# A linear-attention and gated-expert kernel: a new pipeline, k^T v per head in column tiles, and TensorE kept in program order

## The chip, the cores and the metric

The kernel runs on one core of a Trainium2 chip. Its time is the device time of one execution in microseconds (us); the figure quoted is the median of several runs. The traces come from the hardware profiler, one execution each. Five engines work side by side, each through its own instructions in a fixed order: TensorE (PE, with its weight loads as PEld), VectorE (DVE), ScalarE (ACT), GpSimd (POOL), and SyncE (SP), whose queue issues the DMAs here.

## What is computed

Two layers, one behind the other, for 8 batches of 576 tokens.

```python
kv = np.einsum('bhsd,bhse->bhde', k, v)            # 8 heads of 64, no softmax
out = np.einsum('bhsd,bhde->bhse', q, kv)
rms = np.sqrt(np.mean(out * out, axis=-1, keepdims=True) + 1e-06)
x = out / rms * g_norm                             # [8, 576, 512], heads side by side
logits = x @ w_gate                                # 4 experts, the best 2 of them kept
for e in range(E):                                 # w: softmax of the 2 kept logits
    q = x @ wq[e]; k = x @ wk[e]; v = x @ wv[e]    # head size 64
    a = softmax(causal(scale * (q @ k.transpose(0, 2, 1))))
    out += w[..., e] * (a @ v @ wo[e])
```

All four experts are computed for every token; the gate then weighs them.

## The kernel before

The work of a batch has two stages. **Stage 1** (`attention`) makes x. For each of four pairs of heads it transposes q into qT2_all (five blocks of tokens, 128, 128, 128, 128 and 64; `pe_transpose`, line 97), and multiplies k by v for the pair (line 177): a 128x128 product of which only the two 64x64 blocks on the diagonal are wanted. VectorE copies these into kv2_all (lines 186 and 187). Then, block by block of tokens, TensorE makes p_out (line 212, four products in fp32), ScalarE squares it (sq, line 220), VectorE sums (sumsq, line 222) and adds eps (msq, line 229), GpSimd raises to the power -0.5 (rstd, line 238), VectorE scales (x_tok, line 245), TensorE transposes back (p_xT, line 97 again), ScalarE copies it out, and VectorE makes the rounded copy xT_r.

**Stage 2** (`moe_block`) makes the gate from x (p_lt, line 266: fp32 products with only four weight columns, 512 and 64 tokens wide; then p_log, and small VectorE steps), v for all experts (p_v, line 322), and for each of two pairs of experts: q and k projected (p_proj, line 346), scores in causal strips (p_sc, line 371; the two experts of a pair stand in rows 0 to 63 and 64 to 127 and come one behind the other), their exponential (PT, line 378), the triangular mask on GpSimd (line 384), the product with v (p_O, line 409, with one extra column for the sum), its scaling (lines 417 and 418), and the transpose p_OT. The output product p_y (line 455, `moe_final`) of a batch is done within the next one.

`run_interleaved` puts steps of stage 1 of batch b+1 between those of stage 2 of batch b, one for every `ratio` steps. That is the order of the program only: a scheduler then orders each engine's instructions by its own estimates. PSUM, where products land, is one pool of eight one-bank buffers. Loads of a batch go out two batches ahead, in rows of 256 bytes, and the weights are loaded ahead of the first batch.

## Time and profile before

| | |
|---|---|
| median of 3 runs | 517.08 us (516.87 to 517.32) |
| span of the profiled execution | 515.2 us |
| TensorE busy | 400.2 us, 78% |
| VectorE, ScalarE, GpSimd busy | 197.3, 173.9, 124.2 us |
| mean granted TensorE clock | 0.838 of full speed |
| DMA | 40.31 MB, 78 GB/s over the span |

The time of a run is some 2 us more than the span, which goes from the first to the last instruction. Busy time of TensorE is modelled from the starts of its pipelined products: the distance between the starts of two groups tells more than the length of one. An fp32 product shows as two TensorE instructions (passes): 20 products of p_out a batch are 320 in eight batches. PEclk is the granted share of TensorE's clock: 1.00 is 2.4 GHz, 0.50 is 1.2 GHz.

### The profile page before, as it was taken

To read this page: it belongs to the slowest core of one execution; us is meant where nothing else is said; L and a number is where in the kernel's file an instruction comes from. 1 tells how busy PE (TensorE), PEld (TensorE's weight loads), DVE (VectorE), ACT (ScalarE), POOL (GpSimd) and SP (SyncE) were. 2 spreads that over 40 slices of the span, in tenths; PEclk is the share of its full clock that TensorE was granted. 3 is DMA by queue.
4 is the path that set the end of the run, shared out by engine and by line. 5 is a ranking of instruction groups with operands and counts; after the bars stand their busy time and mean duration, and the time that the engine had idled before them with its cause. 6 is when DMAs were issued, how large, how long until landed. Compare 5 with 4: busy or idle time off the path is not lost.

```text
span 515.2 us, 7111 instructions
## 1 busy us (share of the span) xinstructions
PE 400.2 (78%) x2472; PEld 285.5 (55%) x2472; DVE 197.3 (38%) x717; ACT 173.9 (34%) x569; POOL 124.2 (24%) x234
## 2 busy tenths in 40 slices
PE   0066696959969899679968799679968799679884
PEld 0055285726758467554757368454757367564661
DVE  1104334354252342543443442543433542543523
ACT  0013143611514215252246215251245215251440
POOL 3004202430132302351043302351043302340220
PEclk9999799869955599797988699796988699796866
DMA  8999908801390015900295014900200011000202
GB/s 168 206 195 204 206 13 160 118 1 42 108 205 15 2 41 128 199 2 0 92 182 96 1 41 119 207 3 0 87 7 1 1 42 52 0 2 1 93 0 92
DMA packets 125107, 40.31 MB, mean 78 GB/s; under 512 B 120208, under 2 KB 120208, under 8 KB 125072
## 3 DMA queue, kind: packets, MB, share of 16 engines
q1 hardware_dynamic: 125072, 39.87, 38.8%
q8 instruction: 19, 0.31, 0.3%
q14 instruction: 16, 0.13, 0.1%
HBM read 30.42 MB, written 9.44 MB: 77 GB/s over the span
## 4 chain that ended last, share of the span: by engine, by line
PE 56%; DVE 13%; POOL 11%; ACT 8%; issue 5%; DMA 3%; SPq 3%; POOLq 0%; DVEq 0%; ACTq 0%
POOL rstd L238 11%; PE p_kv L177 10%; PE p_lt L266 9%; PE p_proj L346 9%; PE p_out L212 5%; PE p_v L322 4%; PE p_qT L97 4%; DVE O_sc L418 4%; PE p_O L409 4%; PE p_y L455 3%; DVE x_tok L245 3%; PE p_sc L371 3%; ACT PT L378 3%; DVE sumsq L222 3%; ACT sq L220 2%
## 5 line engine op out<-in xcount | busy, mean ns | idle before, releaser
L384 POOL TENSOR_SCALAR_AFFINE_SELECT PT<-PT 128x128 bf16<-128x128 bf16 (+1 forms) x160 | 44.0, 290 | 195.4 <-ACT PT L378 191.0
L238 POOL TENSOR_TENSOR rstd<-msq,neg_half 128x8 f32<-128x8 f32 (+1 forms) x40 | 65.8, 1645 | 102.3 <-DVE msq L229 98.8
L378 ACT ACTIVATE PT<-p_sc 128x64 bf16<-128x64 f32 (+5 forms) x288 | 65.1, 341 | 14.5 <-PE p_sc L371 13.8
L409 PE MATMUL p_O<-vext,PT 128*128 128x65 bf16 (+2 forms) x480 | 43.5, 232 | 22.0 <-DVE x_tok L245 20.3
L371 PE MATMUL p_sc<-qTp,kTp 64*128 64x64 f32 (+5 forms) x288 | 49.3, 305 | 6.7 <-ACT kTp L358 4.2
L212 PE MATMUL p_out<-kv_all,qT_all 128*128 128x128 f32 (+1 forms) x320 | 52.8, 318 | 2.1 <-ACT PT L378 2.1
L245 DVE TENSOR_TENSOR x_tok<-p_out,rstd 128x512 f32<-128x512 f32 (+1 forms) x40 | 27.6, 689 | 65.3 <-POOL rstd L238 65.3
L177 PE MATMUL p_kv<-v_b,k_b 128*128 128x128 f32 (+1 forms) x320 | 51.7, 300 | 0.0
L97 PE MATMUL p_OT<-ident_b,O_sc 128*128 128x128 bf16 (+1 forms) x80 | 21.8, 273 | 38.4 <-DVE O_sc L418 38.1
L97 PE MATMUL p_qT<-ident_f,q_b 128*128 128x128 f32 (+1 forms) x160 | 28.6, 288 | 29.1 <-DMA q_b<-in_q_dram 29.1
L266 PE MATMUL p_lt<-xT,wg_f 128*4 128x64 f32 (+1 forms) x128 | 50.9, 564 | 0.0
L418 DVE TENSOR_SCALAR O_sc<-p_O,invr,gate 128x64 bf16<-128x64 f32 (+1 forms) x160 | 49.8, 334 | 1.6 <-PE p_OT L97 0.6
L409 PEld LDWEIGHTS <-PT 128*128 128x128 bf16 (+2 forms) x480 | 31.8, 124 | 30.8 <-POOL PT L384 11.1
L371 PEld LDWEIGHTS p_sc<-qTp,kTp 64*128 64x128 f32 (+1 forms) x288 | 39.3, 188 | 16.0 <-ACT kTp L358 5.8
L212 PEld LDWEIGHTS p_out<-kv_all,qT_all 128*128 128x128 f32 (+1 forms) x320 | 44.8, 209 | 5.8 <-ACT PT L378 3.5
L220 ACT ACTIVATE sq<-p_out 128x512 f32<-128x512 f32 (+1 forms) x40 | 23.8, 596 | 66.4 <-PE p_out L212 58.9
L222 DVE TENSOR_REDUCE sumsq<-sq 128x8 f32<-128x512 f32 (+1 forms) x40 | 27.2, 680 | 47.8 <-ACT sq L220 47.8
L177 PEld LDWEIGHTS p_kv<-v_b,k_b 128*128 128x128 f32 (+1 forms) x320 | 41.5, 194 | 6.3 <-issue 0.2
L174 ACT COPY qT_all<-p_qT 128x512 f32<-128x512 f32 x64 | 23.0, 419 | 61.5 <-PE p_qT L97 61.5
L186 DVE COPY kv_all<-p_kv 64x64 f32<-64x64 f32 x32 | 6.9, 216 | 90.1 <-PE p_kv L177 87.3
L97 PEld LDWEIGHTS p_qT<-ident_f,q_b 128*128 128x128 f32 (+1 forms) x160 | 19.4, 143 | 37.4 <-DMA q_b<-in_q_dram 19.9
L97 PE MATMUL p_xT<-ident_f,x_tok 128*128 128x128 f32 (+1 forms) x160 | 30.8, 330 | 8.7 <-DVE x_tok L245 5.8
(53 smaller groups left out, 419.9 us busy)
## 6 DMA issues: line engine op xcount, KB each, us to landing
q_b<-in_q_dram SPq DMA_DIRECT2D x32, 256.0 KB, 5.0
k_b<-in_k_dram SPq DMA_DIRECT2D x32, 256.0 KB, 5.0
v_b<-in_v_dram SPq DMA_DIRECT2D x32, 256.0 KB, 5.1
out_dram<-y_sb SPq DMA_DIRECT2D x32, 256.0 KB, 2.1
q_b<-in_q_dram SPq DMA_DIRECT2D x8, 128.0 KB, 5.1
k_b<-in_k_dram SPq DMA_DIRECT2D x8, 128.0 KB, 4.8
v_b<-in_v_dram SPq DMA_DIRECT2D x8, 128.0 KB, 4.4
out_dram<-y_sb SPq DMA_DIRECT2D x8, 128.0 KB, 2.3
```

Of the source, the lines that this page charges most:

```text
L97: nc.tensor.transpose(out_ap, in_ap, ident[:npart, :npart])
L177: nc.tensor.matmul(p_kv[:, :], lhsT=kb[:nt, i, 2 * hp : 2 * hp + 2, :].rearrange("p h d -> p (h d)"), rhs=vb[:nt, i, 2 * hp : 2 * hp + 2, ...
L212: nc.tensor.matmul(p_out[:nt, hp * P : (hp + 1) * P], lhsT=qT2_all[:, hp, t0 : t0 + nt], rhs=kv2_all[:, hp, :], start=True, stop=True,)
L238: nc.gpsimd.tensor_tensor(out=rstd[:nt, :], in0=msq[:nt, :], in1=neg_half[:nt, :], op=AluOpType.pow,)
L245: nc.vector.tensor_tensor(out=x_tok[:nt, :].rearrange("p (h d) -> p h d", h=H), in0=p_out[:nt, :].rearrange("p (h d) -> p h d", h=H), in1= ...
L266: nc.tensor.matmul(p_lt[:, :], lhsT=wg_f[:, c, :], rhs=xT_sb[:, c, slo:shi], start=(c == 0), stop=(c == NCH - 1),)
L346: nc.tensor.matmul(p_proj[:, :], lhsT=wsrc[:, c, 2 * pr : 2 * pr + 2, :].rearrange("p e f -> p (e f)"), rhs=xT_r[:, c, plo:phi], start=(c ...
L371: nc.tensor.matmul(p_sc[:nk, :], lhsT=kT_pair[pb : pb + Hd, t0 : t0 + nk], rhs=qT_pair[pb : pb + Hd, lo:hi], start=True, stop=True,)
L378: nc.scalar.activation(PT[:nk, off + (lo - t0) : off + (hi - t0)], p_sc[:nk, :], ACTF.Exp, scale=scale,)
L384: nc.gpsimd.affine_select(out=PT[:nk, off : off + nk], in_=PT[:nk, off : off + nk], compare_op=AluOpType.is_ge, fill=0.0, base=0, pattern= ...
L409: nc.tensor.matmul(p_O[:nq, :], lhsT=PT[:nkk, col : col + nq], rhs=v_ext[:nkk, kbi, e, :], start=(kbi == 0), stop=(kbi == qci),)
L418: nc.vector.tensor_scalar(out=O_sc[:nq, el, :], in0=p_O[:nq, 0:Hd], scalar1=invr[:nq], scalar2=gate[:nq, qci, e : e + 1], op0=AluOpType.mu ...
```

## The change

The kernel body is rewritten; shapes, data types and results stay. The core of the diff for stage 1 and the loads:

```diff
-    ps = ctx.enter_context(tc.tile_pool(name="ps", bufs=8, space=bass.MemoryType.PSUM))
...
+    ps2 = ctx.enter_context(tc.tile_pool(name="ps2", bufs=3, space=bass.MemoryType.PSUM))
+    ps1 = ctx.enter_context(tc.tile_pool(name="ps1", bufs=2, space=bass.MemoryType.PSUM))
+
+    def big(name):
+        return ps2.tile([P, 2, 512], FP32, tag="big", name=name)
+
+    def small(shape, name, dtype=FP32):
+        return ps1.tile(shape, dtype, tag="small", name=name)
...
+            main(kt, k, h0, h0 + step)
+            main(vt, v, h0, h0 + step)
+            if h0 == 0:
+                rem(kr[b % 2], k)
+                rem(vr[b % 2], v)
+        for i, (t0, nt) in enumerate(blocks):
+            nc.sync.dma_start(
+                qt[:nt, i, :, :], q[b, :, t0 : t0 + nt, :].rearrange("h p d -> p h d")
+            )
+        return qt, kt, vt
...
+    loads = {0: load_qkv(0, fine=True)}
...
+    def kv_pair(p_kv, c, kb, vb, krem, vrem):
+        for j in range(NF + 1):
+            for hh in range(2):
+                h = 2 * c + hh
+                lk, rv = (kb[:, h, j, :], vb[:, h, j, :]) if j < NF else (krem[:, h, :], vrem[:, h, :])
+                nc.tensor.matmul(
+                    p_kv[hh * Dh : (hh + 1) * Dh, c, :], lhsT=lk, rhs=rv,
+                    start=(j == 0), stop=(j == NF), skip_group_check=True,
+                )
+
+    def kv_copy(p_kv, kvb, kv2):
+        for hh in range(2):
+            pp = slice(hh * Dh, (hh + 1) * Dh)
+            nc.vector.tensor_copy(out=kvb[pp, :, hh, 0:Dh], in_=p_kv[pp, :, :])
+            nc.scalar.copy(kv2[pp, :, hh * Dh : (hh + 1) * Dh], p_kv[pp, :, :])
...
+        p_kv = small([P, NCH, Dh], "p_kv")
+        for c in range(NCH):
+            kv_pair(p_kv, c, kb, vb, kr[b % 2], vr[b % 2])
+        kv_copy(p_kv, kvb, kv2)
+        yield 4.3
...
+        p_kt = small([P, NCH, P], "p_kt")
+        for c in range(NCH):
+            nc.tensor.transpose(p_kt[:, c, :], kv2[:, c, :], ident_f[:])
+        kt_sb = s1.tile([P, NCH, P], FP32, tag="kvT", name="kvT")
+        nc.vector.tensor_copy(out=kt_sb[:], in_=p_kt[:])
+        yield 0.5
+        q_block(1)
+        yield 0.5
...
+        for c in range(NCH):
+            nc.tensor.matmul(
+                p_kg[:, c, :, :].rearrange("p a e -> p (a e)"),
+                lhsT=kt_sb[:, c, :],
+                rhs=wg_bd[:, c, :, :].rearrange("p a e -> p (a e)"),
...
+        nc.vector.tensor_copy(out=kvb[:, :, :, Dh:GW], in_=p_kg[:])
+        yield 0.9
...
-            p_kv = psum([P, P], name="p_kv")
-            for i, (t0, nt) in enumerate(blocks):
-                nc.tensor.matmul(
-                    p_kv[:, :],
-                    lhsT=kb[:nt, i, 2 * hp : 2 * hp + 2, :].rearrange(
...
-                    rhs=vb[:nt, i, 2 * hp : 2 * hp + 2, :].rearrange("p h d -> p (h d)"),
...
-            nc.vector.tensor_copy(kv2_all[0:Dh, hp, 0:Dh], p_kv[0:Dh, 0:Dh])
-            nc.vector.tensor_copy(kv2_all[Dh:P, hp, Dh:P], p_kv[Dh:P, Dh:P])
...
-            p_lt = psum([E, shi - slo], name="p_lt")
+            p_o = big("p_out")
             for c in range(NCH):
                 nc.tensor.matmul(
-                    p_lt[:, :],
-                    lhsT=wg_f[:, c, :],
-                    rhs=xT_sb[:, c, slo:shi],
-                    start=(c == 0),
-                    stop=(c == NCH - 1),
-                )
...
-            pe_transpose(p_log[:nt, i, :], lgT[:, t0 : t0 + nt], E)
...
+                    p_o[:nt, c // 2, (c % 2) * 2 * GW : (c % 2 + 1) * 2 * GW],
+                    lhsT=qT[:, c, t0 : t0 + nt],
+                    rhs=kvb[:, c, :, :].rearrange("p a g -> p (a g)"),
+                    start=True,
+                    stop=True,
+                )
...
+            sq = sqs[i % 3]
+            nc.scalar.activation(
+                sq[:nt, :, 0:Dh].rearrange("p (k h) d -> p k h d", k=2),
+                po[:, :, :, 0:Dh],
+                ACTF.Square,
+                scale=1.0 / (Dh**0.5),
...
+            ms = blk.tile([P, H], FP32, tag="ms", name="ms")
+            nc.vector.tensor_reduce(ms[:nt], sq[:nt], axis=AX_X, op=AluOpType.add)
+            rstd = blk.tile([P, H], FP32, tag="rstd", name="rstd")
+            nc.gpsimd.tensor_tensor(
+                out=rstd[:nt], in0=ms[:nt], in1=neg_half[:nt], op=AluOpType.pow
+            )
...
+            nc.vector.tensor_tensor(
...
+            gl = blk.tile([P, H, E], FP32, tag="gl", name="gl")
+            nc.vector.tensor_tensor(
...
+            nc.vector.tensor_reduce(
+                lg8[:nt, i, 0:E],
...
+            pend.append((i, xt))
+            yield 0.9
+            if len(pend) > 1:
+                x_flush()
+                yield 0.45
+        while pend:
+            x_flush()
+            yield 0.45
```

k and v of 512 tokens now come in rows of 1024 bytes, four tokens to a partition (the sum over tokens doesn't mind their order), the last 64 tokens in zero-filled tiles of their own, so every product of line 175 has 128 rows. There are 40 of them a batch instead of 20, each 64 weight columns by 64 moving columns, the heads of a pair in turns in the two column halves of the array. The gate's weights are folded in: p_kt transposes kv, p_kg multiplies by the gate weights, and p_out gets 136 columns instead of 128, the eight more of which are the logits per head; gl and lg8 scale and add them. p_lt, p_log, msq and the second copy of xT are gone. VectorE copies qT, ScalarE copies y.

Stage 2 computes the same products: the projections in two halves of 288 tokens instead of 512 and 64, 24 score products a batch instead of 36, the two experts of a pair in turns into two banks, so that one exponential serves both (10 a batch instead of 36) and one mask too (10 instead of 20). The rest, and what sets the order:

```diff
+            def piece(parts):
+                p_s = big("p_sc")
+                o = 0
+                for kb, lo, hi in parts:
+                    for el in range(2):
+                        pb = slice(el * Hd, (el + 1) * Hd)
                         nc.tensor.matmul(
...
+                            p_s[:, el, o : o + hi - lo],
+                            lhsT=kTp[pb, kb * P : (kb + 1) * P],
+                            rhs=qTp[pb, lo:hi],
...
+                d0 = strip_off[kb] + lo - kb * P
...
+        def pv(pr):
+            PT = res["PT", pr]
+            p_O = big("p_O")
...
+                for n, qc in enumerate(qcs):
...
+                for sub in ((qcs,) if bank == 0 else ((3,), (4,))):
...
+                    iv = inv[:nq, sub[0] : sub[0] + nn, :]
+                    nc.vector.reciprocal(iv.rearrange("p n e -> p (n e)").unsqueeze(2), po[:, :, Hd : Hd + 1])
+                    nc.vector.tensor_tensor(
+                        out=iv, in0=iv, in1=gate[:nq, sub[0] : sub[0] + nn, 2 * pr : 2 * pr + 2],
+                        op=AluOpType.mult,
...
+                    nc.vector.tensor_tensor(
+                        out=osc[:nq, sub[0] : sub[0] + nn, :, :].rearrange("p n e f -> p (n e) f"),
+                        in0=po[:, :, 0:Hd],
+                        in1=iv.rearrange("p n e -> p (n e)").unsqueeze(2).to_broadcast([nq, 2 * nn, Hd]),
+                        op=AluOpType.mult,
                     )
...
+        def o_t(pr):
+            osc = res["osc", pr]
+            p_t = small([P, S], "p_OT", BF16)
...
+                nc.tensor.transpose(
+                    p_t[:, s0 : s0 + nq],
+                    osc[:nq, qc, :, :].rearrange("p e f -> p (e f)"),
...
+            nc.scalar.copy(OT[:, pr, :], p_t[:])
+            yield 0.5
+
+        yield from proj(0)
+        yield from scores(0)
+        yield from proj(1)
+        yield from scores(1)
+        if prev_y is not None:
+            yield from prev_y
+        yield from pv(0)
+        yield from o_t(0)
+        yield from pv(1)
+        yield from o_t(1)
+        res["OT"] = OT
...
+            p_y = small([P, D], "p_y")
...
+            nc.scalar.copy(y[:nq, :], p_y[:nq, :])
...
+    W1, W2 = 16.0, 17.0
+
+    def weave(main, side):
+        a = s = 0.0
+        live = side is not None
+        for c in main:
+            a += c / W2
+            while live and s < a:
                 try:
-                    next(gen_side)
+                    s += next(side) / W1
...
+    with tc.manual_schedule(engines={mybir.EngineType.PE}):
...
+            weave(stage2(b, res, y_gen), stage1(b + 1, nxt) if b + 1 < B else None)
```

`weave` goes by the costs that the steps yield. `manual_schedule` keeps TensorE's instructions in program order; the other engines are still ordered by the scheduler. PSUM is now three buffers of two banks (big) and two of one bank (small).

Three places show the new order, each before and then changed. First VectorE in stage 1 of a batch while stage 2 of the one before it runs (invr, O_sc and osc belong to stage 2). Before:

```order
L222 TENSOR_REDUCE sumsq<-sq 128x8
L417 RECIPROCAL invr<-p_O 128x1 x2
L229 SCALAR_TENSOR_TENSOR msq<-sumsq,eps_row 128x8
L418 TENSOR_SCALAR O_sc<-p_O,invr,gate 128x64
L245 TENSOR_TENSOR x_tok<-p_out,rstd 128x512
L418 TENSOR_SCALAR O_sc<-p_O,invr,gate 128x64
L222 TENSOR_REDUCE sumsq<-sq 128x8
```

Changed, for the second and third block of a batch:

```order
L266 TENSOR_REDUCE ms<-sq_120 128x8
L273 TENSOR_TENSOR x_tok<-p_out,rstd 128x512
L280 TENSOR_TENSOR gl<-p_out,rstd 128x32
L286 TENSOR_REDUCE lg_0_102<-gl 128x4
L308 MAX m_2312<-lg_0_102 128x8
L446 RECIPROCAL inv<-p_O 128x6
L266 TENSOR_REDUCE ms<-sq_122 128x8
L447 TENSOR_TENSOR inv<-inv,gate 128x6
L451 TENSOR_TENSOR osc<-p_O,inv 128x384
L273 TENSOR_TENSOR x_tok<-p_out,rstd 128x512
```

In both, the sum for a block stands behind x_tok of the block ahead of it; three small steps of the gate now stand between them.

Second, TensorE at the end of stage 1 of batch 0. Before:

```order
L212 MATMUL p_out<-kv_all,qT_all 128x128 x4
L97 MATMUL p_xT<-ident_f,x_tok 128x128 x4
L212 MATMUL p_out<-kv_all,qT_all 64x128 x4
L97 MATMUL p_xT<-ident_f,x_tok 128x128 x8
L97 MATMUL p_xT<-ident_f,x_tok 128x64 x4
L266 MATMUL p_lt<-xT,wg_f 4x512 x4
L266 MATMUL p_lt<-xT,wg_f 4x64 x4
```

Changed:

```order
L250 MATMUL p_out<-kvx_98,qT 128x136 x4
L242 MATMUL p_x<-ident_f,x_tok 128x128 x4
L250 MATMUL p_out<-kvx_98,qT 64x136 x4
L242 MATMUL p_x<-ident_f,x_tok 128x128 x4
L242 MATMUL p_x<-ident_f,x_tok 128x64 x4
L333 MATMUL p_v<-wv_r,xT 128x256 x4
L175 MATMUL p_kv<-v_b,k_b 64x64 x8
```

p_v, and behind it all of k^T v of the next batch, now follow the last transpose of x directly. In later batches the five transposes p_OT of the second pair stand between the last two p_x.

Third, the DMAs that SyncE's queue issues first. Before:

```order
L110 DMA g_wide<-in_g_norm_dram 64x1 x2
L118 DMA w_stage<-in_moe_wq_dram 128x4x64 x4
L127 DMA wg_f<-in_moe_w_gate_dram 128x4x4
L135 DMA wo_f<-in_moe_wo_dram 128x512 x2
L151 DMA q_b<-in_q_dram 128x8x64
L118 DMA w_stage<-in_moe_wk_dram 128x4x64 x4
L151 DMA k_b<-in_k_dram 128x8x64
L151 DMA v_b<-in_v_dram 128x8x64
```

Changed, from the last two loads of k and v of batch 0 on:

```order
L112 DMA k_b<-in_k_dram 128x2x256
L112 DMA v_b<-in_v_dram 128x2x256
L130 DMA q_b<-in_q_dram 128x8x64 x4
L130 DMA q_b<-in_q_dram 64x8x64
L139 DMA g_wide<-in_g_norm_dram 64x1 x2
L141 DMA wg_st<-in_moe_w_gate_dram 128x4x4
L154 DMA w_stage<-in_moe_wv_dram 128x4x64 x4
```

Batch 0 comes ahead of the weights, and k and v ahead of q.

## Rows read from the trace of the kernel before

**Rows 1.** The page: busy time, share and instructions of each engine.

```profile
PE 400.2 (78%) x2472; PEld 285.5 (55%) x2472; DVE 197.3 (38%) x717; ACT 173.9 (34%) x569; POOL 124.2 (24%) x234
```

**Rows 2.** One steady batch by stretches: start:end, length, busy (x count) by engine, PEclk.

```profile
239.60:266.90 27.30, 24.21 (x176) 18.81 (x174) 10.81 (x39) 10.34 (x37) 4.47 (x12) 1.00 0.43 100
...
266.90:273.70 6.80, 4.50 (x30) 3.57 (x26) 3.83 (x19) 0.97 (x2) 1.64 (x1) 0.50 1.19 203
...
273.70:287.40 13.70, 10.37 (x69) 8.43 (x69) 5.46 (x16) 8.95 (x30) 8.26 (x14) 1.00 0.25 47
...
287.40:297.60 10.20, 9.08 (x42) 3.48 (x41) 4.09 (x20) 1.17 (x3) 1.19 (x2) 0.50 0.01 2
```

**Rows 3.** The same view of the loading, stage 1 of batch 0, the last batch; GB/s last.

```profile
0.00:31.20 31.20, 2.14 (x5) 0.91 (x5) 3.09 (x5) 1.87 (x2) 4.47 (x16) 1.00 0.96 186
...
41.20:58.50 17.30, 8.56 (x62) 7.03 (x60) 8.83 (x21) 5.32 (x9) 8.76 (x6) 0.91 1.16 197
...
472.80:515.20 42.40, 32.71 (x191) 22.39 (x188) 17.36 (x66) 13.20 (x53) 5.39 (x20) 0.73 0.16 56
```

**Rows 4.** Timeline (start, length, instruction): the gate product of batch 0 and of batch 4.

```profile
58.51 5.69 PE L266 MATMUL p_lt<-xT,wg_f 128*4 128x512 f32 x14
...
292.51 6.55 PE L266 MATMUL p_lt<-xT,wg_f 128*4 128x512 f32 x16
```

**Rows 5.** Timeline: the normalisation of one block in stage 1, and its last step.

```profile
43.09 0.69 DVE L222 TENSOR_REDUCE sumsq<-sq 128x8 f32<-128x512 f32 x1 [1.27 <-ACT sq L220]
...
43.82 0.17 DVE L229 SCALAR_TENSOR_TENSOR msq<-sumsq,eps_row 128x8 f32<-128x8 f32 x1
...
44.14 1.65 POOL L238 TENSOR_TENSOR rstd<-msq,neg_half 128x8 f32<-128x8 f32 x1 [39.04 <-DVE msq L229]
...
45.82 0.69 DVE L245 TENSOR_TENSOR x_tok<-p_out,rstd 128x512 f32<-128x512 f32 x1 [1.15 <-POOL rstd L238]
...
57.09 0.68 DVE L245 TENSOR_TENSOR x_tok<-p_out,rstd 64x512 f32<-64x512 f32 x1 [1.53 <-POOL rstd L238]
```

**Rows 6.** Timeline: TensorE groups in pairs, a group and the one right behind it.

```profile
241.90 1.57 PE L322 MATMUL p_v<-wv_r,xT_r 128*128 128x256 f32 x11
...
243.31 0.80 PE L97 MATMUL p_qT<-ident_f,q_b 128*128 128x128 f32 x5
...
244.04 1.57 PE L177 MATMUL p_kv<-v_b,k_b 128*128 128x128 f32 x10
...
245.54 1.20 PE L322 MATMUL p_v<-wv_r,xT_r 128*128 128x256 f32 x8
...
251.21 1.56 PE L346 MATMUL p_proj<-xT_r,wq_r 128*128 128x512 f32 x8
...
252.61 0.86 PE L97 MATMUL p_qT<-ident_f,q_b 128*128 128x128 f32 x5
...
256.77 1.04 PE L371 MATMUL p_sc<-qTp,kTp 64*128 64x512 f32 x6 [0.31 <-ACT kTp L358]
...
257.74 0.86 PE L97 MATMUL p_qT<-ident_f,q_b 128*128 128x128 f32 x5
...
260.58 1.16 PE L212 MATMUL p_out<-kv_all,qT_all 128*128 128x128 f32 x8
...
261.67 0.69 PE L371 MATMUL p_sc<-qTp,kTp 64*128 64x256 f32 x5
```

**Rows 7.** Groups by form: count, busy us and mean ns of one, idle before.

```profile
L177 PE MATMUL p_kv<-v_b,k_b 128*128 128x128 f32 x256 | 38.4, 294 | 0.0
...
L418 DVE TENSOR_SCALAR O_sc<-p_O,invr,gate 128x64 bf16<-128x64 f32 x128 | 40.4, 336 | 1.3 <-PE p_OT L97 0.6
...
L309 DVE TENSOR_TENSOR gate<-gt,rden 128x20 f32<-128x20 f32 x8 | 1.4, 177 | 0.2
```

**Rows 8.** Timeline: the second pair of experts in the last batch.

```profile
490.74 2.77 PE L346 MATMUL p_proj<-xT_r,wq_r 128*128 128x512 f32 x8
...
496.10 3.39 PE L371 MATMUL p_sc<-qTp,kTp 64*128 64x512 f32 x18 [0.21 <-ACT kTp L358]
```

More of the change, by code (lines that the diff above doesn't have):

```diff
@@ L38 @@
     D = H * Dh
-    E, D2, Hd = moe_wq.shape
-    assert D2 == D, (D2, D)
-    assert D % P == 0
-    assert 2 * Dh == P, "head dim must be 64 for head-pairing"
-    assert H % 2 == 0 and E % 2 == 0
+    E, _, Hd = moe_wq.shape
+    assert (P, H, S, Dh, E, Hd) == (128, 8, 576, 64, 4, 64)
     NCH = D // P
-    HP = H // 2
     EP = E // 2
-    scale = 1.0 / (Hd**0.5)
-    blocks = []
-    t0 = 0
-    while t0 < S:
-        nt = min(P, S - t0)
-        blocks.append((t0, nt))
-        t0 += P
-    NB = len(blocks)
@@ L319, in moe_block @@
+        nc.vector.tensor_tensor(out=gate[:], in0=gt[:], in1=rden[:].unsqueeze(2).to_broadcast([P, NB, E]), op=AluOpType.mult)
+        vx = vexts[b % 2]
         for i, (t0, nt) in enumerate(blocks):
-            p_v = psum([P, E * Hd], name="p_v")
+            p_v = small([P, E * Hd], "p_v")
             for c in range(NCH):
@@ L454, in moe_final, with final @@
+        yield from scores(1)
[6 more added lines that the diff above has]
+        res["OT"] = OT
+    def final(b, OT):
+        for qc, (s0, nq) in enumerate(blocks):
+            p_y = small([P, D], "p_y")
             for pr in range(EP):
                 nc.tensor.matmul(
[L456 to L458 removed]
@@ L459, in moe_final @@
[L459 to L475 removed]
+                    p_y[:nq, :], lhsT=OT[:, pr, s0 : s0 + nq], rhs=wo_b[:, pr, :],
@@ L505 @@
-    for _ in deferred:
-        pass
+                    live = False
+        if live:
+            for _ in side:
+                pass
+    with tc.manual_schedule(engines={mybir.EngineType.PE}):
+        res = {}
+        for _ in stage1(0, res):
+            pass
+        y_gen = None
+        for b in range(B):
+            if b + 2 < B:
+                loads[b + 2] = load_qkv(b + 2)
+            nxt = {}
+            weave(stage2(b, res, y_gen), stage1(b + 1, nxt) if b + 1 < B else None)
+            y_gen = final(b, res["OT"])
+            res = nxt
+        for _ in y_gen:
+            pass
```

588 lines of the change are left out of this document (234 added, 354 removed).

## The prediction

> **What bounds the kernel now.** I read the busy times first, then the steady batch in stretches, then the timeline of its TensorE work, and last the two ends. TensorE is busy 78% of the span [rows 1], and no other engine is over 38%. A batch lasts 58.5 us: p_lt of batch 0 starts at 58.51, of batch 4 at 292.51 [rows 4], and (292.51 - 58.51) / 4 = 58.5. Within one, TensorE is busy 24.2 of 27.3, 4.5 of 6.8, 10.4 of 13.7 and 9.1 of 10.2 us, 48.2 of 58.0 in all [rows 2]. So about 10 us a batch are waits, and the rest is work, 17 us of it at 1.2 GHz: the second and fourth stretch have PEclk 0.50, after the products p_O, where TensorE works in short pieces [rows 2]. The bound is TensorE, by its amount of work, by its clock and by a few waits. At the ends, the first 31 us go to loading, at 186 GB/s with TensorE busy 2.1 us; stage 1 of batch 0 then takes 17.3 us from its first p_out on, with nothing beside it; and the last batch takes 42.4 us from the end of its gate product [rows 3].
>
> **The change: TensorE's work.** Distances between group starts [rows 6] give the present paces at full clock. p_v: 11 products in 243.31 - 241.90 = 1.41 us, 0.13 each. Transposes: five in 0.73. p_kv: ten passes in 1.50. p_proj: eight in 1.40. Scores: six, of 1344 columns (512, 384, 256 and three of 64), in 0.97, 0.72 ns a column. p_out: eight passes in 1.09.
>
> I split the new batch where its first p_out is issued, since TensorE's order is now fixed. The **first half** runs from p_v up to there, and holds:
> - p_v, 20 products by 0.13: 2.6.
> - k^T v, 80 passes of half the weight columns and half the moving columns instead of 40. If both shrink a pass alike, it costs 75 ns and the whole 6.0, as before. No row shows such passes. Below lies 3.0, if the two column halves work at the same time; above lies 12.0, if a pass keeps its 150 ns. The pass is nearest to the present one with everything halved, and the narrow pass behind the 64-token tail goes, so I take 5.0.
> - Projections: as many columns and products as now, 4 x 1.40 = 5.6 at most. The 64-column products among the eight, which cost more than their columns, are gone: 1.2 each, 4.8.
> - Scores: 6400 columns a batch by 0.72 ns are 4.6; half of that if the two row halves work at once; I take 3.3 for what lies ahead of p_out.
> - 20 transposes of q: 2.6. p_kt 0.5, p_kg 0.6 (eight passes on eight columns, a little under p_out's).
> - Waits: the scores need kT, which ScalarE must copy behind the last projection; now 0.31 us of idle [rows 6], with one longer copy and nothing between 0.9, and 0.4 for the second pair; 0.7 for the two small PSUM buffers behind p_kv. In all 2.0.
>
> That is 21.4 us. ScalarE keeps up: ten long exponentials replace 36.
>
> p_lt goes, 5.7 to 6.6 us a batch with its start at the low clock [rows 4]. But the place is taken by p_v and k^T v, which follow the sparse end of the other half. The dense run from 292.51 to 297.6 was still at 0.50 [rows 2, 4], 5.1 us, half of it lost. So 2.5 more: **24 us**, with ends of 18 and 31.
>
> **The change: the other half is a chain.** From the first p_out on, five blocks pass p_out, Square, sum, power, x_tok, p_x, and the order of VectorE decides the pace: the sum of a block stands behind x_tok, gl, lg8 and max of the block ahead. A block costs VectorE's sum 0.69; from the end of the small step ahead of the power to x_tok 45.82 - 43.99 = 1.83; x_tok 0.69 [rows 5]; and three steps like the gate's, 0.18 each [rows 7], 0.5: 3.7. Five blocks, up to the last x_tok, are 18.0. Behind block 3 stand six steps of osc (0.18 to 0.34 each [rows 7]), 1.15, since p_O's results are scaled by the same engine; behind block 4 another 0.85. The first p_out and its Square add 1.8. After the last x_tok, VectorE has the last osc steps, 1.9, and TensorE, which has p_OT in front of the last p_x, another 0.5. Sum **24.2 us**. In it lie, hidden, about 13 us of TensorE work: p_y, p_O, p_out, p_x. GpSimd's masks and ScalarE's copies of y are hidden as well; uncovered, the y copies would cost five by 0.6. Present blocks come at (57.09 - 45.82) / 4 = 2.8 us [rows 5], which gives 20 as the lower end; with each block waiting 1 us for TensorE or ScalarE, 29 is the upper.
>
> A batch is thus 24 + 24 = 48 us instead of 58.5. The first, which has no y in it, 47.
>
> **The change: the ends.** Batch 0 now comes ahead of the weights. Its 3.54 MB (q, k and v, each 8 heads x 576 tokens x 64 x 4 bytes) take 19.0 us at 186 GB/s [rows 3]; with some 2 us for the first issue and the last landing q is whole at 21. VectorE's scaling of wv stands in its queue ahead of the first sum and waits for 0.52 MB more, 2.8 us, and takes 0.75; with its landing that is 25.3. Five blocks at 3.3 (the gate's steps hide under the power here) and the last transpose give 42.3 for the first p_v, where p_lt now starts at 58.5. Batch 1's k and v come at about 43, hardly in the way. Ends: 37 and 47.
>
> The Trainium skill, DMA: Bandwidth & Descriptors, Specifications, puts 512 bytes as the least transfer for line rate. All large loads of the stretch are of 256-byte rows but for the output weights, so no row here shows it; if k and v went twice as fast by it, the head would lose 5 us more, and the sum would be 410.
>
> In the last batch the second pair's projections come before p_O of the first; now 496.10 - 490.74 = 5.4 us pass in them, cold and alone [rows 8]. Most of that, 3, goes under the exponentials; fewer instructions and four y buffers give another 3: 36 instead of 42.4 (32 to 40).
>
> **Sum.** 42.3 + 47 + 6 x 48 + 36 = 413 us of span, and 517.1 - 515.2 = 1.9 outside it: **415 us**.
>
> **Rivals.** *The halves work side by side.* If column and row halves of the array run at once, k^T v falls by 2 us and the scores by 1; if TensorE then stays at its full clock, 2.5 more; with blocks at the present 2.8 us, 4 more. All of it takes 9.5 off each of seven batches, 415 - 66 = 349; the half of it gives 382. For it: p_out's passes stream without a gap now. Against: the order of VectorE is fixed, and nothing of it shortens the power. The Trainium skill, TensorEngine Tiling (Array Packing), Key Properties, says that different tiles can load and multiply in parallel; no row here shows two tiles in turns. By that rule alone k^T v would be 3.0 and the scores 2.3, 21 us less in all, 394, which is within the forecast's case.
>
> *Program order waits.* A fixed order can't fill gaps; two small buffers and three big ones, and p_O waiting behind a late x_tok, could add 8 us a batch: 56, and 415 + 7 x 8 = 471. For it: TensorE waits some 10 us a batch now, though the scheduler fills in. Against: I have counted the waits that I can see.
>
> *Column tiles don't overlap, slower.* If each pass of k^T v waits for its weights and the weights for the pass ahead in the other half, it costs the whole 294 ns of the present one [rows 7], 23.5 us for 80 instead of 5: 18.5 more in each of seven batches, 415 + 7 x 18.5 = 545. The time before is reached at 517 - 415 = 102 us, 14.6 a batch, a pass of (5 + 14.6) / 80 = 245 ns. Against: present passes of twice the size come each 150.
>
> **How the numbers follow.** Forecast, a batch of 44 to 53: 66%. Shorter by halves side by side, under 385: 15%. Waits, 450 to 510: 13%. Column tiles slow, over 518: 5%; within 0.2% of the time before, about what a measurement of this kernel can tell from no change: 1%. The range leaves out half of the waits' case, the slow one and the far end of the short one: 370 to 458. Faster 0.94, same 0.01, slower 0.05.
>
> **What would show it.** Starts of p_v of successive batches 48 us apart; first p_v near 42; k^T v of a batch near 5 us at full clock; x_tok of a batch 3.7 to 5 us apart with VectorE waiting on the power; TensorE idle some 3 us ahead of the first p_OT and 4 ahead of the second, and PEclk at 0.50 about there. I am wrong if x_tok come closer together, if k^T v takes over 9 us, or if TensorE has long waits in the first half.

## The result and the profile of the changed kernel

The changed kernel takes 407.9 us (median of 4 runs, 406.6 to 410.2), the kernel before 517.0 in the same comparison: a ratio of 0.791, interval 0.787 to 0.795. The forecast was 415, range 370 to 458. The profiled execution took 408.3 us, of which 406.6 are span. Of the experiments below, e4 and e6 had two and three of their four runs in a disturbed, slower state, their traces among them; only the others count as times, 410.3 and 416.3 us for e4 and 372.1 for e6.

The page of the changed kernel, its busy line for [rows 1]:

```profile
PE 301.0 (74%) x2616; PEld 245.7 (60%) x2624; DVE 162.6 (40%) x513; ACT 154.9 (38%) x273; POOL 103.3 (25%) x146
```

TensorE has 99 us less of work, and the span shrank by 109: of its idle time, 115 us before, 106 are left. Where they lie is read from the stretches, in the columns of [rows 2] (start:end, length, busy and count by engine, PEclk, DMA share, GB/s). The first two are batch 0, the next four a steady batch:

```profile
44.90:65.35 20.45, 18.70 (x185) 16.15 (x184) 8.13 (x21) 8.32 (x16) 2.28 (x6) 0.88 1.04 273
65.35:97.23 31.88, 18.70 (x134) 15.40 (x134) 12.34 (x44) 8.37 (x14) 9.60 (x9) 0.68 0.23 47
...
233.19:238.23 5.04, 5.04 (x84) 4.75 (x84) 0.43 (x1) 0.22 (x1) 0.00 (x0) 0.57 0.01 3
238.23:253.37 15.14, 13.38 (x104) 11.12 (x100) 6.45 (x13) 7.83 (x14) 2.27 (x6) 1.00 0.52 157
253.37:264.00 10.63, 6.90 (x53) 5.00 (x55) 5.07 (x15) 6.56 (x12) 5.19 (x7) 1.00 0.84 210
264.00:278.44 14.44, 10.67 (x90) 8.90 (x90) 7.82 (x36) 4.49 (x9) 4.40 (x3) 0.76 0.05 10
```

The first half of a batch, from p_v to the first p_out, is dense: 18.4 of 20.2 us. The second holds 17.6 us of TensorE work in 25.1 us, and in batch 0 18.7 in 31.9. TensorE idles 7.5 us in this steady second half and 13 in that of batch 0.

VectorE and TensorE in that steady second half (timeline: start, length, engine, line, instruction, and in brackets the idle time ahead and what ended it). First VectorE:

```profile
257.81 0.69 DVE L273 TENSOR_TENSOR x_tok<-p_out,rstd 128x512 f32<-128x512 f32 x1 [1.82 <-POOL rstd L268]
...
261.46 0.69 DVE L273 TENSOR_TENSOR x_tok<-p_out,rstd 128x512 f32<-128x512 f32 x1 [1.82 <-POOL rstd L268]
...
263.46 0.56 DVE L451 TENSOR_TENSOR osc<-p_O,inv 128x384 bf16<-128x384 f32 x1
265.17 0.69 DVE L273 TENSOR_TENSOR x_tok<-p_out,rstd 128x512 f32<-128x512 f32 x1 [1.15 <-POOL rstd L268]
...
268.83 0.69 DVE L266 TENSOR_REDUCE ms<-sq 128x8 f32<-128x520 f32 x1 [1.25 <-ACT sq L259]
271.34 0.69 DVE L273 TENSOR_TENSOR x_tok<-p_out,rstd 128x512 f32<-128x512 f32 x1 [1.81 <-POOL rstd L268]
```

Then TensorE, the same time:

```profile
264.07 0.40 PE L431 MATMUL p_O<-vext,PT 128*128 128x65 bf16 x8 [2.76 <-DVE osc L451]
...
265.98 2.18 PE L250 MATMUL p_out<-kvx,qT 128*128 128x136 f32 x8
```

Two blocks come 3.65 and 3.71 us apart, as forecast, with VectorE waiting 1.82 us for the power in the first interval, and in the second 1.15, since osc takes up the rest. The third interval is 6.17. There VectorE waits for a Square (268.83), the Square for p_out (265.98), and that p_out stands in TensorE's order behind products of p_O's second bank, which wait until osc of the first bank is through (263.46 + 0.56 = 264.02). The two banks share no data; p_O is one tile, and in the program the scaling of bank one is written ahead of the products of bank two. Part of the interval is the clock: PEclk is 0.50 from 266.0 to 269.9, after that wait, and the eight passes of p_out at 265.98 take 2.0 us up to the next group, where those at 259.75 took 1.0.

Batch 0 shows it more strongly, having no p_y between its blocks. TensorE:

```profile
71.33 0.60 PE L431 MATMUL p_O<-vext,PT 128*128 128x65 bf16 x8 [3.98 <-DVE osc L451]
71.74 2.16 PE L250 MATMUL p_out<-kvx,qT 128*128 128x136 f32 x8
...
79.10 0.23 PE L463 MATMUL p_OT<-ident_b,osc 64*128 64x64 bf16 x1 [2.56 <-DVE osc L451]
...
80.29 2.16 PE L250 MATMUL p_out<-kvx,qT 128*128 128x136 f32 x8
```

The second, third and fourth p_out stand behind a product that waits for osc (the fourth behind 1.53 us at 84.53), and the osc of the first two of these waits stands on VectorE behind x_tok of the block before. x_tok comes at 69.79, 77.62, 85.63, 92.42 and 96.04.

### The profile page after: what moved, and what is told of

Read it like the earlier page. It is cut to its first block, busy times and chain, and to the rows that moved or that the text cites. A ratio compares the mean times of both kernels' runs of the same rounds, so it can differ in the third digit from the quotient of the medians.

```text
span 406.6 us, 6644 instructions
## 1 busy us (share of the span) xinstructions
PE 301.0 (74%) x2616; PEld 245.7 (60%) x2624; DVE 162.6 (40%) x513; ACT 154.9 (38%) x273; POOL 103.3 (25%) x146
## 5 line engine op out<-in xcount | busy, mean ns | idle before, releaser
L268 POOL TENSOR_TENSOR rstd<-ms,neg_half 128x8 f32<-128x8 f32 (+1 forms) x40 | 66.0, 1649 | 115.3 <-DVE ms L266 88.3
L394 POOL TENSOR_SCALAR_AFFINE_SELECT PT<-PT 128x256 bf16<-128x256 bf16 (+1 forms) x80 | 29.8, 383 | 167.5 <-ACT PT L389 166.7
L250 PE MATMUL p_out<-kvx,qT 128*128 128x136 f32 (+1 forms) x320 | 58.1, 337 | 0.7
L389 ACT ACTIVATE PT<-p_sc 128x576 bf16<-128x576 f32 (+3 forms) x80 | 51.6, 707 | 11.8 <-PE p_sc L379 11.8
L250 PEld LDWEIGHTS p_out<-kvx,qT 128*128 128x128 f32 (+1 forms) x320 | 50.2, 222 | 7.1 <-PE p_x L242 2.5
L273 DVE TENSOR_TENSOR x_tok<-p_out,rstd 128x512 f32<-128x512 f32 (+1 forms) x40 | 27.6, 690 | 66.4 <-POOL rstd L268 66.4
L242 PE MATMUL p_x<-ident_f,x_tok 128*128 128x128 f32 (+1 forms) x160 | 31.0, 331 | 20.7 <-DVE gl L280 16.9
L201 DVE COPY qT<-p_q 128x512 f32<-128x512 f32 (+1 forms) x40 | 25.5, 638 | 42.3 <-PE p_q L196 41.7
L333 PE MATMUL p_v<-wv_r,xT 128*128 128x256 f32 (+1 forms) x160 | 31.8, 342 | 6.4 <-DVE vext L340 3.6
L266 DVE TENSOR_REDUCE ms<-sq 128x8 f32<-128x520 f32 (+1 forms) x40 | 27.2, 679 | 22.9 <-ACT sq L259 22.9
L175 PE MATMUL p_kv<-v_b,k_b 128*64 128x64 f32 x512 | 31.5, 296 | 6.0 <-DMA v_b<-in_v_dram 6.0
L175 PEld LDWEIGHTS p_kv<-v_b,k_b 128*64 128x64 f32 x512 | 28.2, 207 | 8.0 <-issue 7.0
```

The lines of the kernel that those rows point to most:

```text
L175: nc.tensor.matmul(p_kv[hh * Dh : (hh + 1) * Dh, c, :], lhsT=lk, rhs=rv, start=(j == 0), stop=(j == NF), skip_group_check=True,)
L242: nc.tensor.transpose(p_x[:, c, :nt], xt[:nt, c * P : (c + 1) * P], ident_f[:nt, :nt])
L250: nc.tensor.matmul(p_o[:nt, c // 2, (c % 2) * 2 * GW : (c % 2 + 1) * 2 * GW], lhsT=qT[:, c, t0 : t0 + nt], rhs=kvb[:, c, :, :].rearrange(" ...
L266: nc.vector.tensor_reduce(ms[:nt], sq[:nt], axis=AX_X, op=AluOpType.add)
L268: nc.gpsimd.tensor_tensor(out=rstd[:nt], in0=ms[:nt], in1=neg_half[:nt], op=AluOpType.pow)
L273: nc.vector.tensor_tensor(out=xt[:nt].rearrange("p (k h d) -> p k h d", k=2, h=4), in0=po[:, :, :, 0:Dh], in1=rb.to_broadcast([nt, 2, 4, Dh]),
```

## The experiments

All start from the changed kernel, 407.9 us. Theory A at first: the second half is a chain through VectorE and GpSimd, with waits of TensorE for osc on top. The main rival: TensorE's work sets the pace everywhere.

**e1, the power twice.**

```diff
-            nc.gpsimd.tensor_tensor(out=rstd[:nt], in0=ms[:nt], in1=neg_half[:nt], op=AluOpType.pow)
+            for _ in range(2):
+                nc.gpsimd.tensor_tensor(out=rstd[:nt], in0=ms[:nt], in1=neg_half[:nt], op=AluOpType.pow)
```

> GpSimd raises every block's sums to the power twice, into the same tile; nothing else is added. Theory A (the half from the first p_out on is a chain through the power): each of the 40 blocks comes 1.65 us later, 66 us in all, 474; somewhat less, down to 460, where a block waits for TensorE anyway. Rival B (TensorE's amount of work sets the pace, and GpSimd with 25% busy time has room): under 15 us more, below 423.

463.6 us (462.8 to 463.9), 55.7 more, 1.39 for each of 40 blocks. The steady blocks of e1 (VectorE's timeline):

```profile
241.79 0.69 DVE L274 TENSOR_TENSOR x_tok<-p_out,rstd 128x512 f32<-128x512 f32 x1 [3.48 <-POOL rstd L269]
247.11 0.69 DVE L274 TENSOR_TENSOR x_tok<-p_out,rstd 128x512 f32<-128x512 f32 x1 [3.48 <-POOL rstd L269]
```

They are 5.32 apart, 1.67 more than 3.65, and the wait went from 1.82 to 3.48. In these blocks GpSimd, busy 25% of the time in the changed kernel, is on the path with the whole of its power; over all blocks it is 1.39 of 1.65 us. The rival falls.

**e2, osc of the first bank behind the products of the second.**

```diff
                     yield 0.11 * (qc + 1)
+            for bank, qcs in groups:
                 for sub in ((qcs,) if bank == 0 else ((3,), (4,))):
```

> The scaling of the first bank of p_O is written behind the products of the second bank, for both pairs; all work stays. In the changed kernel the second bank's products wait 2.76 us for osc in a steady batch, and 3.98 and 1.53 us in batch 0, with the next block's p_out queued behind them. Theory A (these waits are on the path): the block intervals of 6.2 us in a steady batch and of 7 to 8 us in batch 0 fall to about 4; 2 to 2.5 us less in each of six batches and 5 in the first, 388 (385 to 395). Rival B (the wait only moves, to the p_OT behind it or to VectorE): within 5 us of 408.

425.6 us (423.9 to 426.8): slower by 17.7, where both theories expected less time or the same. TensorE in a steady batch of e2:

```profile
267.52 0.77 PE L431 MATMUL p_O<-vext,PT 128*128 128x65 bf16 x20
...
273.60 0.34 PE L464 MATMUL p_OT<-ident_b,osc 128*128 128x128 bf16 x3 [2.04 <-DVE osc L452]
...
277.50 0.23 PE L464 MATMUL p_OT<-ident_b,osc 64*128 64x64 bf16 x1 [2.55 <-DVE osc L452]
...
279.34 2.02 PE L250 MATMUL p_out<-kvx,qT 128*64 128x136 f32 x8
```

The wait inside p_O is gone, and the first intervals are 3.65, 3.65 and 4.18. But all osc steps now come late, p_OT waits for them (61.8 us over the run; 14.0 in the changed kernel), and the p_out of the last block stands behind p_OT: its x_tok comes 8.5 us after the one ahead. So the wait is not a property of p_O. In a fixed order, whatever waits for osc holds up the next block, and the theory became: **the fixed order on TensorE turns VectorE's delays into waits for ready work**. e5 tests it.

**e3, k^T v twice.** Each `kv_pair(...)` call stands twice.

> Every product of k^T v is made twice, into the same place. Theory A (the first half of a batch is TensorE's work, a pair of passes costs what their starts show): 80 more passes at 49 ns are 3.9 us in each of seven batches, and under 1 in the first, where loading decides: 436; if the added work lies at full clock, 2.4 each, 425. Rival B (the first half waits for ScalarE's and VectorE's copies): under 5 us more.

422.0 us (419.9 to 423.4): 14.1 more, 2.0 in each of seven batches. That is near the second figure of Theory A (2.4 each): the added passes come at the full clock, at 29 ns each (below), which makes 2.3. The first half is bound by TensorE for the most part.

**e4, the two heads not in turns.**

```diff
-        for j in range(NF + 1):
-            for hh in range(2):
+        for hh in range(2):
+            for j in range(NF + 1):
```

> The two heads of a pair no longer take turns in the column halves: the ten passes of one head come first, then those of the other. Same products. Theory A (passes in turns start almost together, 6 ns and then 100 ns at half clock, 3 and then 54 at full; one half alone would keep the 100 or 54 ns for every pass): k^T v 8 us instead of 3.9 at half clock, or 4.3 at full; 2 to 4 us more in each of seven batches, 422 to 436. Rival B (the pitch is set by the weight loads, whichever half they go to): within 3 us of 408.

410.3 and 416.3 us; against the kernel before 0.796, interval 0.786 to 0.806, which overlaps with that of the changed kernel. The time doesn't decide. The trace gives the pace. At half clock (e4; v_rem and k_rem are the last two of a head's ten passes):

```profile
193.13 0.31 PE L175 MATMUL p_kv<-v_rem,k_rem 128*64 128x64 f32 x1
193.19 0.31 PE L175 MATMUL p_kv<-v_b,k_b 128*64 128x64 f32 x1
193.24 0.31 PE L175 MATMUL p_kv<-v_rem,k_rem 128*64 128x64 f32 x1
```

Passes of one head start 107 ns apart at half clock and 58 at full (starts in e4's trace), nearly as Theory A said of one half alone. But the heads are not quite apart: the next head, in the other half, starts beside the last three passes of the head ahead (193.19 lies between 193.13 and 193.24). So ten passes take 0.70 us at half clock and 0.40 at full, 70 and 40 ns each. In turns (changed kernel):

```profile
234.34 1.12 PE L175 MATMUL p_kv<-v_b,k_b 128*64 128x64 f32 x16
235.25 0.43 PE L175 MATMUL p_kv<-v_rem,k_rem 128*64 128x64 f32 x4
...
237.55 0.63 PE L175 MATMUL p_kv<-v_b,k_b 128*64 128x64 f32 x16
238.02 0.28 PE L175 MATMUL p_kv<-v_rem,k_rem 128*64 128x64 f32 x4
```

Sixteen passes take 235.25 - 234.34 = 0.91 us at half clock, 57 ns each, and 0.47 at full, 29 each. That is half of 107 and of 58: in turns the two column halves work fully side by side. e4 loses less than Theory A gave because it keeps part of that overlap.

**e5, TensorE ordered by the scheduler.**

```diff
-    with tc.manual_schedule(engines={mybir.EngineType.PE}):
+    if True:
```

> The changed kernel with TensorE's instructions ordered by the scheduler, as those of the other engines are; nothing else differs. Theory A (part of the gain is the fixed order: k^T v and q transposes fill the first half and the second half is the chain in any case): slower, 415 to 440. Rival B (the fixed order costs, since p_out stands behind products that wait for osc; the scheduler puts ready work there): 385 to 400.

370.8 us (369.5 to 372.2), ratio to the kernel before 0.716 (0.712 to 0.720): **37 us faster** than the changed kernel, better than Rival B hoped. Waits (us in all, times, longest) of the changed kernel:

```profile
DVE x_tok L273 <- POOL rstd L268: 66.4, 40, 1.8
...
PE p_O L431 <- DVE osc L451: 33.5, 16, 4.0
...
PE p_x L242 <- DVE gl L280: 16.9, 11, 3.0
...
PE p_OT L463 <- DVE osc L451: 14.0, 15, 2.6
```

The same of e5:

```profile
DVE x_tok L273 <- POOL rstd L268: 54.7, 40, 1.8
PE p_x L242 <- DVE gl L280: 35.2, 28, 2.2
...
PE p_O L431 <- DVE osc L451: 1.8, 8, 0.3
```

And its group of p_OT (count, busy us and mean ns of one, idle ahead and what ended it):

```profile
L463 PE MATMUL p_OT<-ident_b,osc 128*128 128x128 bf16 (+1 forms) x80 | 15.0, 261 | 0.2 <-DVE osc L451 0.2
```

47.5 us of waiting for osc became 2.0. The first p_v comes 2.1 us earlier, batch 0 is 10.4 shorter (42.0 instead of 52.3), the six steady batches 3.4 each (42.0 instead of 45.4), the last 4.7: 37.6 of span. What TensorE waits for now is mostly the chain itself (p_x behind gl, 35.2 us instead of 16.9), so the 47.5 us are not all gain. Nor is all of the gain there. The steady batch of e5 in its two halves (columns of [rows 2]):

```profile
210.33:228.74 18.41, 18.09 (x185) 15.34 (x184) 7.52 (x18) 8.33 (x16) 2.27 (x6) 0.89 0.44 130
228.74:252.24 23.50, 17.23 (x145) 12.90 (x145) 11.48 (x46) 10.53 (x20) 9.59 (x9) 0.92 0.40 101
```

The second half is 1.6 us shorter than 25.1, and the first 1.8 shorter than 20.2: there the scheduler fills TensorE's waits for ScalarE's kT (0.73 and 0.29 us in the changed kernel) and VectorE's vext (0.52).

**e6, the next block ahead, VectorE in program order too.** p_out, Square, sum and power of block i+1 are written ahead of x_tok of block i.

```diff
+        for i in range(NB):
+            done.append((i, *part_a(i)))      # p_out, sq, ms, rstd
+            yield 0.9
+            if len(done) > 1:
+                part_b(*done.pop(0))          # x_tok, gl, lg8
...
-    with tc.manual_schedule(engines={mybir.EngineType.PE}):
+    with tc.manual_schedule(engines={mybir.EngineType.PE, mybir.EngineType.DVE}):
```

> In stage 1 the products p_out, Square, sum and power of the next block are written ahead of x_tok, gl and the sum of the gate of this block, and VectorE too is kept in program order (max of the gate comes at the end of the batch). Theory A (blocks of the second half are a chain of sum, power and x_tok, 3.65 us each, with waits for osc behind it): two blocks overlap, blocks 2.5 us apart; about 5 us less in each of seven batches and 4 in batch 0's stage 1, 370 (360 to 388). Rival B (TensorE's own order and its waits for osc set the pace): within 8 us of 408. Rival C (x_tok now stands behind osc on VectorE, and VectorE's fixed order adds waits): over 415.

372.1 us in one run, within Theory A's range. At the head, where nothing else is queued, the blocks show what the chain is worth (VectorE, e6):

```profile
27.83 0.69 DVE L278 TENSOR_TENSOR x_tok<-p_out,rstd 128x512 f32<-128x512 f32 x1 [0.19 <-POOL rstd L269]
29.44 0.69 DVE L278 TENSOR_TENSOR x_tok<-p_out,rstd 128x512 f32<-128x512 f32 x1
31.52 0.68 DVE L278 TENSOR_TENSOR x_tok<-p_out,rstd 128x512 f32<-128x512 f32 x1
```

They are 1.6 to 2.1 us apart instead of 3.2 to 3.8, and the first p_v starts at 36.3 instead of 44.9. In steady batches two blocks come 1.9 apart, and then p_O's second bank waits for osc again (28.6 us over the run), while VectorE's waits for the power fall from 66.4 us to 1.8. So both losses are real, and this edit takes the one and leaves most of the other.

**e7 and e8, the loads and the column tiles.** e7 loads k and v as before, in 256-byte rows with a token to a partition; e8 does that and makes k^T v by pairs of heads, 128 by 128.

```diff
-                dst[:, h0:h1, :, :].rearrange("p h j d -> p h (j d)"),
-                src[b, h0:h1, 0 : NF * P, :].rearrange("h (p j) d -> p h (j d)", j=NF),
+                dst[:, j, h0:h1, :],                                  # e7: for each j
+                src[b, h0:h1, j * P : (j + 1) * P, :].rearrange("h p d -> p h d"),
...
+                p_kv[:, c, :, :].rearrange("p a d -> p (a d)"),       # e8: both heads at once
+                lhsT=lk.rearrange("p a d -> p (a d)"), rhs=rv.rearrange("p a d -> p (a d)"),
```

> k and v are loaded in rows of 256 bytes, a token to a partition, as in the kernel before; same bytes, same products. Theory A (loading decides only ahead of the first p_out, at some 190 GB/s for short rows): 2 us later at the head, 408 to 413. Rival B (short rows take twice as long): k and v of batch 0 whole some 6 us later, first p_out 5 us later, 413 to 416, and loads of later batches still hidden. Rival C (1 KB rows buy nothing): 408 within 1.5.

> As the last one, but k^T v by pair of heads as in the kernel before: 20 products of 128 weight columns by 128 moving columns (40 passes), of which the two diagonal blocks are copied out. Against the last one, Theory A (a pass of this form took 150 ns at full clock in the kernel before, and most of k^T v now lies at half clock): 6.0 us at full and up to 8 at half clock instead of 3.9: 2 to 4 us more in each of seven batches, 422 to 440. Rival B (a pass is 109 ns at full clock like a transpose of 128 columns, 4.4 a batch): 1 to 2 us more, 415 to 425. Rival C (it's the same, column tiles bring nothing): within 3 us of the last one.

e7: 418.1 us (415.7 to 418.6), 10.2 more, above all three forecasts. Its first p_out comes at 32.67 instead of 23.85, its first p_v 9.1 us later, and its steady batch is the same (45.4), so nearly all of it lies at the head. But it is not the price of short rows alone. SyncE's queue of e7:

```profile
0.80 1.98 SPq L113 DMA_DIRECT2D k_b<-in_k_dram  x4
...
18.76 4.43 SPq L131 DMA_DIRECT2D q_b<-in_q_dram  x5
```

Each of 32 loads of 64 KB takes the queue 0.5 us to issue, 131 GB/s at the most (130 and 126 came from 10 to 20 us), and q is issued at 18.8 instead of 6.6. What is shown is that many small loads cost the head 9 us; what the row length alone costs is open.

e8: 428.5 us (425.0 to 428.7), 10.4 above e7, 1.5 a batch. k^T v in e8:

```profile
251.06 1.91 PE L175 MATMUL p_kv<-v_b,k_b 128*128 128x128 f32 x8
252.76 0.63 PE L175 MATMUL p_kv<-v_rem,k_rem 128*128 128x128 f32 x2
...
255.00 1.06 PE L175 MATMUL p_kv<-v_b,k_b 128*128 128x128 f32 x8
255.90 0.39 PE L175 MATMUL p_kv<-v_rem,k_rem 128*128 128x128 f32 x2
```

Eight passes take 0.90 us at full clock, 112 ns each, and 1.70 at half, 212. Forty of them are 4.5 us at full clock, against 80 by 29 ns = 2.3 in column tiles; as they lie, partly at half clock, 6.1 (251.06 to 257.16) against 3.9. Rival B of e8 was right in the pass and in the 1 to 2 us a batch; its total stood on a faster e7.

**e9 to e12, can both losses go?** e9: the blocks of e6, with both engines ordered by the scheduler. e10: as e9, with smaller yields in front and larger ones for the blocks, so that the first p_out comes among the scores of the first pair. e11: the program of e10 with TensorE and VectorE fixed. e12: the yields of e10 on the changed kernel's own blocks, TensorE free.

```diff
-        yield 4.3                        # behind k^T v; 0.5 -> 0.3, 0.9 -> 0.5 up to p_kg
+        yield 2.5
...
-            yield 0.9                    # a block of p_out; x_flush 0.45 -> 0.6
+            yield 1.35
```

> The next block's p_out, Square, sum and power written ahead of x_tok of this one, as in the run before it of this kind, but with TensorE and VectorE both ordered by the scheduler. Theory A (two separate losses, the wait in TensorE's fixed order and the chain through the power): below both single edits, 340 to 362. Rival B (they are one loss, and either edit takes it): 368 to 374. Rival C (the scheduler puts x_tok ahead of the next sum again, so the edit does nothing on VectorE): as TensorE's free order alone, 371 within 3.

> As the last one, and the costs that the steps of stage 1 yield are changed so that its first p_out comes among the scores of the first pair and the blocks are spread over the rest of the batch; only the order changes. Theory A (TensorE has about 300 us of work at the present clock, and what is left above it are waits in the half with the chain): the chain lies under the scores and projections, 325 to 350. Rival B (the two small and three big PSUM buffers and the order of VectorE hold it back): within 5 of the last one, or slower.

> The same order of the program as the last one, with TensorE and VectorE kept in it. Theory A (a fixed order costs only where ready work stands behind a wait; with the next block ahead and the chain spread out little of that is left): within 8 us of the last one. Rival B (fixed order costs some 37 us whatever the program, as it does in the changed kernel): 25 to 40 us above the last one.

> The changed kernel with the costs of stage 1's steps set so that the first p_out comes among the scores of the first pair, TensorE ordered by the scheduler, and without writing the next block ahead. Theory A (the earlier start of the chain is what brought the gain, and writing ahead made VectorE's order worse): 350 to 362. Rival B (the earlier start gives little, since blocks hold two-bank PSUM buffers that projections and scores want): 366 to 375.

| | us (runs) | ratio to before | steady batch |
|---|---|---|---|
| e9, ahead, free | 382.0 (381.6 to 382.9) | 0.734 (0.729 to 0.739) | 44.3 |
| e10, ahead, early, free | 365.8 (365.1 to 366.3) | 0.703 (0.697 to 0.708) | 40.7 |
| e11, ahead, early, fixed | 392.5 (389.3 to 393.9) | 0.753 (0.747 to 0.760) | 45.2 |
| e12, early, free | 374.0 (371.7 to 376.4) | 0.719 (0.712 to 0.725) | 42.9 |

e9 is Rival C and worse: the scheduler puts x_tok ahead of the next sum again (238.33 and 239.48 in VectorE's timeline), and the last block's x_tok comes 9.3 us after the one ahead. The same text in fixed order, e6, took 372.1 in one run: here the scheduler's order is the slower one. e10 is the fastest of all, 42 us under the changed kernel, and its interval lies just below e5's, but it stays 16 us above the upper end of Theory A, and Rival B was wrong too. No run shows what holds it there; in its trace p_out now waits for the two-bank buffers (8.0 us behind gl), and blocks are still 3.65 us apart in pairs (x_tok at 228.57 and 232.22). e11 against e10 prices the fixed order once more, now of TensorE and VectorE together and on another program: 26.8 us, within Rival B's 25 to 40, though "whatever the program" does not hold, by e6 and e9. e12 shows that the early start alone brings nothing.

## Why the prediction was right, and where it was not

| | forecast | measured |
|---|---|---|
| first p_v | 42.3 | 44.9 |
| batch 0 | 47 | 52.3 |
| six steady batches | 48 each | 45.4 each (45.1 to 45.6) |
| last batch | 36 | 37.2 |
| span | 413 | 406.6 |

The sum is 7 us off because +2.6, +5.3 and +1.2 stand against six times -2.6. That the total came so near is in part luck: it was better than its terms.

**The chain.** Forecast 3.7 us a block and 24.2 us for the half; measured 3.65 and 3.71 where nothing else intervenes, and 25.1. The sum of it was right, one of its steps was not. I put 1.15 us of osc on VectorE behind block 3. These steps hide under the power there (263.46); what makes the interval 6.17 is TensorE's fixed order and the low clock behind its wait. That the half came within 1 us is luck here: the osc steps that I put at 2.0 us cost 0.4 (the last interval is 4.09), and TensorE's order with its clock, which I put at nothing, 2.5. The lower end, 20 us, came from the 2.8 us a block in batch 0 of the kernel before, and I did not say why blocks were closer there. VectorE had the next block's sum ahead of x_tok, under the power:

```profile
43.99 0.69 DVE L222 TENSOR_REDUCE sumsq<-sq 128x8 f32<-128x512 f32 x1
```

That x_tok starts at 45.82 [rows 5]; e6 restores this order.

The osc reading also contradicts the places I named for TensorE's idle time. It idles 2.8 us ahead of p_O's second bank and none ahead of the first p_OT; only the second p_OT waits about where I said, 2.3 us in two pieces. "I have counted the waits that I can see" against the rival of program order was the failing sentence: I had seen waits for osc ahead of p_OT, and not that one tile makes the second bank of p_O wait for the first. By e5 that rival costs 3.4 us in a steady batch and 10.4 in batch 0, where I gave it 8 in every batch; it lost to the other gains and not for want of a mechanism (of the 3.4, 1.8 lie in the first half, where it is waits for kT and vext that are filled). In batch 0 it is twice my error there.

**The first half**, in distances between starts of the batch at 233.19, with TensorE's own waits in them:

| | forecast | measured |
|---|---|---|
| p_v and k^T v, with the cold clock | 2.6 + 5.0 + 2.5 | 4.3 + 3.9 |
| projections with the waits for kT (measured: the first) | 4.8 + 1.3 | 5.3 |
| scores ahead of the first p_out | 3.3 | 2.7 |
| q transposes, p_kt, p_kg, with the second wait for kT | 3.7 | 4.0 |
| wait for small buffers | 0.7 | none apart from p_v's 0.5 |
| together | 24 | 20.2 |

The cold clock came as forecast: PEclk 0.57 over the 5.0 us of p_v and k^T v, behind the sparse second half. My p_kg, 0.6, was read too low from p_out's passes (1.09 for eight); it takes 0.8. What was mis-sized most is the pass of k^T v. I took 5.0 us at full clock, between 3.0 and 12.0; by the passes at full clock it is 2.3, below my lower end, and 3.9 is what it costs mostly at half clock. Two steps were missing. The 150 ns from which I started are a mean that takes in the passes around the 64-token tail; e8, which has no such passes, shows 112. And a pass in turns costs a quarter of that: half for half the moving columns (58 ns, e4), and half again since the column halves work at once (29). The Trainium skill, TensorEngine Tiling (Array Packing), Key Properties, says that tiles load and multiply in parallel, and its Theoretical Speedup gives up to a factor of two for 64 columns; 58 against 29 ns agrees.

The row halves of the scores work at once too. In the last batch nothing stands between the pairs (one product of each expert). The timeline, cut by its window ahead of the first, the second and the third pair:

```profile
376.93 0.74 PE L379 MATMUL p_sc<-qTp,kT 64*128 64x288 f32 x6 [0.73 <-ACT kT L362]
...
377.17 0.50 PE L379 MATMUL p_sc<-qTp,kT 64*128 64x288 f32 x4
...
377.30 0.37 PE L379 MATMUL p_sc<-qTp,kT 64*128 64x448 f32 x2
```

The second pair, twice 288 columns, takes 0.13 us, as long as one product of a projection with 288 columns (eight in 1.05 us, 241.39 to 242.44). What eats the gain is the start and the end of a group: the first pair takes 0.24, and a pair ahead of a product on the whole array 0.1 more than one ahead of another of 64 rows. In a steady batch the scores stand in short groups between transposes and projections, so that 6400 columns take 2.67 us and 0.34 behind the first p_out, 0.47 ns each, no better than the 0.46 of a projection. At 0.13 us for a pair of 288, the 5888 columns ahead of p_out would be 1.3 of the 2.67 us (an estimate); the rest goes to starts and ends of groups. My 3.3 was too high, I think because the narrow products are gone; no run shows that.

So the rival of halves side by side was right about the array and wrong about its worth. The column halves are worth 1.5 us a batch against pairs (e8 less e7; 80 passes at 58 ns would be 4.6 us, as much as 40 at 112), the row halves' gain is lost between short groups, and the closer blocks that it hoped for did not come: they stayed at 3.65.

**The head.** VectorE's scaling of wv, forecast to end at 25.3, ends at 24.42 + 0.75 = 25.2. The first sum comes only at 26.68, behind its Square, and the blocks are 3.6 apart where I took 3.3, since wq's and wk's scaling and the gate's steps don't all hide:

```profile
24.42 0.75 DVE L155 TENSOR_SCALAR wv_r<-w_stage,g_wide 128x1024 fp32r<-128x1024 f32 x1
26.68 0.69 DVE L266 TENSOR_REDUCE ms<-sq 128x8 f32<-128x520 f32 x1 [1.51 <-ACT sq L259]
29.15 0.69 DVE L273 TENSOR_TENSOR x_tok<-p_out,rstd 128x512 f32<-128x512 f32 x1 [1.77 <-POOL rstd L268]
...
43.49 0.68 DVE L273 TENSOR_TENSOR x_tok<-p_out,rstd 64x512 f32<-64x512 f32 x1 [1.81 <-POOL rstd L268]
```

That is 1.4 and 1.1 of the 2.6 us. The loads in 1 KB rows ran faster than the 186 GB/s that I took for all: 299 GB/s from 5 to 10 us, against 160 to 170 from 13 to 23, with q's 256-byte rows. The Trainium skill, DMA: Bandwidth & Descriptors, Specifications, asks 512 bytes for line rate, and the two rates agree with it. No run varies the row length alone, though, and q's rows reach 224 GB/s in e7, from 20 to 25 us. The 5 us that I gave for that case did not come: p_kg waits 1.28 us for VectorE's scaling of the gate's weights, whose load stands behind q in the queue, and starts at 19.66; the last q transposes stand behind it at 21.36.

**The last batch** took 37.2 against 36; no run splits the two savings of 3 that I put there.
